# Eighteen weight pieces laid 2,080 bytes apart instead of 2,048

## The chip, the cores and the metric

The kernel runs on one core of one Trainium2 chip. The metric is the device time of that core in microseconds (us), taken as the median of several runs. Data lives in three places: the chip's main memory, the on-chip working memory (128 partitions, each a row of bytes with its own addresses), and the accumulators that TensorE (PE) writes. VectorE (DVE), ScalarE (ACT) and GpSimd (POOL) work beside PE, and SyncE (SP) issues the transfers. PEld in the profile is PE's loading of weights, which goes on beside its matmuls.

## The reference

The program computes an attention with two kinds of masks, and then a feed-forward layer that takes the largest of three products:

```python
scores = scale * np.matmul(q, k.transpose(0, 1, 3, 2))      # q, k, v: 8 x 8 heads x 576 x 64
scores = np.where(masks[None, :, :, :], scores, -1000000000.0)
attn = np.exp(scores - np.max(scores, axis=-1, keepdims=True))
attn = attn / (np.sum(attn, axis=-1, keepdims=True) + 1e-09)
x = np.matmul(attn, v)                                       # turned to 4608 tokens x 512
h = np.maximum(np.maximum(x @ w1, x @ w2), x @ w3)           # 512 -> 768, three times
out = h @ w_out                                              # 768 -> 512
```

Heads 0 to 3 look back over a window of 32 positions, heads 4 to 7 over 32 positions that lie 4 apart. q, k, v and the output are float32; the four weight matrices come as float64, each number in two words of 32 bits.

## The kernel before, in words

**Stages.** The 4,608 tokens are worked through in nine tiles of 512. Attention makes the columns of x for a tile (in "units" of one half sequence and a pair of heads), and the feed-forward layer of the tile follows. A planner with costs and due times writes all instructions in one order ahead of time, so that the attention of the next tile is woven into the matmuls of this one. For the last two tiles no attention is left.

**Two parts for each operand.** To get near to float32 accuracy from a fast matmul, x, the weights and h are each held as a high part and a low remainder, in a float32 form that PE takes at its faster rate (fp32r, shown as f32 in the rows). A product is three products: high x by high weights, low x by high weights, high x by low weights.

**The up product** (function `ffn`, L828) is the largest part. For each tile, each of six blocks f of 128 hidden columns and each of the three weight matrices g, there are 3 terms times 4 chunks c of 128 inputs: 12 matmuls, 1,944 over the kernel. The weights of a chunk (128 columns, 512 bytes in each partition) are loaded as the stationary operand, and 512 tokens of xH or xL (2,048 bytes in each partition) stream past. Every matmul has a weight load of its own, which runs beside the matmul ahead of it.

**The down product** (L883) has 648 matmuls of the same size. There h is the stationary operand, and the weights wdn stream past.

**Where the up weights lie.** Two tiles, wupH and wupL, hold the high and the low parts. Each has 18 pieces, number j = 3f + g, and a piece is 4 chunks of 512 bytes, one behind the other. The pieces are written once: the float64 words of a piece are brought into a staging tile st by a transfer, made into one float32 each on DVE, ACT and POOL, then cast into wupH (ACT, L346, once DVE, L350) and the remainder subtracted into wupL (POOL, L353). The function `weight` does it; `copy` and `tt` are the helpers whose lines the rows show.

**Addresses.** Tiles that stay for the whole kernel are laid out in order of their making, one behind the other in each partition: ident, identb, masks, wupH, wupL, xH, xL, and then all others. In the built program the starts are these (bytes in each partition, and the remainder by 512 in brackets):

| tile | start before | start after |
|---|---|---|
| masks, identb | 1,920 (384) and 1,664 (128) | the same |
| wupH, piece j | 2,944 + 2,048 j (384) | 2,944 + 2,080 j (384 + 32 j) |
| wupL, piece j | 39,808 + 2,048 j (384) | 40,384 + 2,080 j (448 + 32 j) |
| xH, chunk c | 76,672 + 5,120 c (384) | 77,824 + 5,120 c (0) |
| xL, chunk c | 97,152 + 5,120 c (384) | 98,304 + 5,120 c (0) |
| wdn, the first | 153,376 (288) | 154,528 (416) |
| h, the first | 177,952 (288) | 179,104 (416) |

All the wdn tiles have the remainder 288 before, and all the h tiles too. A matmul starts inside x at a multiple of 1,024 bytes from its chunk's start, and inside wdn or h at a multiple of 512.

Of the kernel before, what the change touches and what calls it, by code (L numbers as in the profile page):

```python
# [9 lines left out]
F32R = mybir.dt.float32r  # L10
# [12 lines left out]
NPAIR = H // 2  # L23
NF = DF // 128
BLOCK = 256
RING = 5 * BLOCK
NEG = -8e9
REBIAS = 2.0**-112
TICK = 10.24 / 3
TILES = [2 * BLOCK] * 9  # L30

# [230 lines left out]
def tile_dilated_window_attention__then__maxout_ffn(  # L262
# [18 lines left out]
    const = ctx.enter_context(tc.tile_pool(name="const", bufs=1))  # L281
# [6 lines left out]

    masks = const.tile([128, 4, 128], BF16, name="masks")
    mask = masks[:, 1]  # L290
    wupH = const.tile([128, 3 * NF, 4, 128], F32R, name="wupH")
    wupL = const.tile([128, 3 * NF, 4, 128], F32R, name="wupL")
    xH = const.tile([128, NPAIR, RING], F32R, name="xH")
    xL = const.tile([128, NPAIR, RING], F32R, name="xL")

# [24 lines left out]
    def buf(tag, name, shape=None, dtype=None):  # L320
        if tag in BANKS:
            return Buf(ps, tag, BANKS[tag], [128, 512], F32, name)
        if tag in KEPT:
            return Buf(KEPT[tag], tag, len(KEPT[tag]), None, None, name)
        n, sh, dt = SIZES[tag]
        return Buf(work, tag, n, shape or sh, dtype or dt, name)
# [17 lines left out]
    def copy(eng, dst, src):  # L344
        if eng == "act":
            nc.scalar.copy(dst, src)  # L346
        elif eng == "pool":
            nc.gpsimd.tensor_scalar(dst, src, 1.0, 1.0, ALU.mult, ALU.mult)
        else:
            nc.vector.tensor_copy(dst, src)  # L350
# [5 lines left out]
    def act(n, psum=True):  # L356
        return (0.155 if psum else 0.195) + 0.00084 * n

    def dve(n):
        return 0.15 + 0.00105 * n  # L360

    def dve2(n):
        return 0.15 + 0.00053 * n

    def pool1(n):
        return 0.17 + 0.00093 * n

    def pool(n):
        return 0.08 + 0.00245 * n
# [6 lines left out]
    def weight(j, before):  # L376

        up = j < NWU
        n = 512 if up else 256
        if not up:  # L380
            f, n0 = (j - NWU) // 2, n * ((j - NWU) % 2)
        tag = STAGE[j % len(STAGE) if j < STAGE_H else 0] if up else "o"
        st = buf(tag, f"st{j}", [128, 2 * n], F32)
        res = [] if up else [wdn[f]]

        def part(z):
            if up:
                return (wupL if z else wupH)[:, j].rearrange("p c m -> p (c m)")
            return wdn[f].t[:, z, n0 : n0 + n]

        cb, cp = buf("tmp", f"c{j}"), buf("b", f"cp{j}")

        def high():
            return st.t.rearrange("p (n t) -> p n t", t=2)[:, :, 1]

        def cf():
            return cb.t[:, :n]

        def cw():
            return cb.t.bitcast(U32)[:, :n]  # L400

        def pf():
            return cp.t[:, :n]

        def pw():
            return cp.t.bitcast(U32)[:, :n]

        def rebias(e):  # L410

            if e == "act":
                nc.scalar.mul(pf(), high(), REBIAS)
            else:
                nc.vector.tensor_scalar(pf(), high(), REBIAS, None, ALU.mult)

        def low3(e):

            b = st.t.bitcast(U8).rearrange("p (n t) -> p n t", t=8)[:, :, 3]
            (nc.gpsimd if e == "pool" else nc.vector).tensor_scalar(cw(), b, 1 / 32, -31 / 64, ALU.mult, ALU.add)  # L420

        def joined(_):

            nc.vector.scalar_tensor_tensor(
                pw(), pw(), 3, cw(), op0=ALU.logical_shift_left, op1=ALU.bitwise_or
            )

        def split(e):
            copy(e, part(0), cf())

        def sign(_):
            nc.vector.scalar_tensor_tensor(
                cw(), st.t.bitcast(U32).rearrange("p (n t) -> p n t", t=2)[:, :, 1], 0x80000000, pw(), op0=ALU.bitwise_and, op1=ALU.bitwise_or
            )

        s = plan.add(
            {"sp": 0.5},
            lambda _: nc.sync.dma_start(out=st.t.bitcast(I64), in_=w_up[j] if up else w_dn[j - NWU]),
            bufs=[st],
            nbytes=128 * 8 * n,  # L440
        )
        first = plan.add({"act": act(n, False), "dve": dve(n)}, rebias, [s, before], [st, cp])
        s = plan.add({"pool": pool1(n), "dve": dve(n)}, low3, [s, before], [st, cb])
        s = plan.add({"dve": dve(n)}, joined, [s, first], [cp, cb])
        s = plan.add({"dve": dve(n)}, sign, [s], [st, cp, cb])
        s = plan.add({"act": act(n, False), "dve": dve2(n), "pool": pool1(n)}, split, [s], [cb, *res])
        l = plan.add(
            {"pool": pool(n), "dve": dve(n)},
            lambda e: tt(e, part(1), cf(), part(0).bitcast(F32), ALU.subtract),
            [s],  # L450
            [cb, *res],
        )
        return s, l, first
# [160 lines left out]
    def rounded_of(half, p, dil, pv):  # L614

        r0 = (half * HALF) % RING
        cut = min(HALF, RING - r0)
        parts = [(0, cut, r0)] + ([(cut, HALF, 0)] if cut < HALF else [])
# [184 lines left out]
    def ffn(t0, n, x_of, w_of, prev):  # L803

        r0 = t0 % RING
        turned = r0 + n > RING

        def moving(x, c):

            if turned:  # L810
                return x[:, c].rearrange("p (b k) -> p b k", k=BLOCK)[:, 0 : RING // BLOCK : RING // BLOCK - 1]
            return x[:, c, r0 : r0 + n]

        def sums(bank):
            return bank.t[:, :n].rearrange("p (b k) -> p b k", k=BLOCK) if turned else bank.t[:, :n]

        halves = range(t0 // HALF, -(-(t0 + n) // HALF))
        hs, hsteps = [], []
        for f in range(NF):
            tmp, hb = buf("tmp", f"tmp{t0}_{f}"), buf("h", f"h{t0}_{f}")  # L820
            for g in range(3):
                bank = buf("ffn", f"u{t0}_{f}_{g}")
                terms = ((wupH, 0, 0), (wupH, 0, 1), (wupL, 1, 0))
                for m, (wt, wz, xz) in enumerate(terms):

                    def up(_, m=m, wt=wt, xz=xz, f=f, g=g, bank=bank):
                        for c in range(4):
                            nc.tensor.matmul(  # L828
                                sums(bank),
                                wt[:, 3 * f + g, c, :],  # L830
                                moving(xL if xz else xH, c),
                                start=(m == 0 and c == 0),
                                stop=(m == 2 and c == 3),
                            )

                    prev = plan.add(
                        {"pe": 4 * (n * 0.000425 + 0.01)},
                        up,
                        [
                            prev,  # L840
                            *(x for h in halves for p in range(NPAIR) for x in x_of[h, p][xz]),
                            w_of[3 * f + g][wz],
                        ],
                        [bank],
                    )
                if g == 0:
                    s = plan.add(
                        {"act": act(n), "dve": dve(n)},
                        lambda e, bank=bank, tmp=tmp: copy(e, tmp.t[:, :n], bank.t[:, :n]),
                        [prev],  # L850
                        [bank, tmp],
                    )
                else:
                    s = plan.add(
                        {"dve": dve(n)},
                        lambda e, bank=bank, tmp=tmp: tt(e, tmp.t[:, :n], bank.t[:, :n], tmp.t[:, :n], ALU.max),
                        [prev, s],
                        [bank, tmp],
                    )
            a = plan.add(  # L860
                {"act": act(n, False), "dve": dve2(n), "pool": pool1(n)},
                lambda e, tmp=tmp, hb=hb: copy(e, hb.t[:, 0, :n], tmp.t[:, :n]),
                [s],
                [tmp, hb],
            )
            l = plan.add(
                {"pool": pool(n), "dve": dve(n)},
                lambda e, tmp=tmp, hb=hb: tt(
                    e, hb.t[:, 1, :n], tmp.t[:, :n], hb.t[:, 0, :n].bitcast(F32), ALU.subtract
                ),  # L870
                [a],
                [tmp, hb],
            )
            hs.append(hb)
            hsteps.append((a, l))
        last_up = prev
        for s0 in range(0, n, 128):
            bank, o = buf("ffn", f"d{t0}_{s0}"), buf("o", f"o{t0}_{s0}")
            for f in range(NF):
# [25 lines left out]
                {"sp": 0.5},  # L905
                lambda _, q0=t0 + ((s0 + BLOCK) % n if turned else s0), o=o: nc.sync.dma_start(out=out[q0 : q0 + 128], in_=o.t),
                [s],
# [116 lines left out]
```

## Time and profile before

| | |
|---|---|
| median of three runs | 722.84 us (722.43 to 723.27) |
| the profiled execution | 724.2 us, of which 722.3 us lie between its first and last instruction |
| mean granted clock of PE | 0.990 |
| PE busy, of the span | 99% |
| DVE, ACT, POOL busy | 51%, 41%, 32% |

The busy time of PE alone says little, since matmuls are pipelined and the shown end of each is modelled: a matmul is shown as 389 ns long while the next one starts 227 ns later. The distance between the starts of matmuls is therefore the thing to read, and the chain of waits, which follows the work that ended last back to the start.

### The profile page before, as it was taken

The numbers are of one execution on the slowest core, as the hardware profiler recorded it, in microseconds if no ns is written. First come the engines' busy times: TensorE is split into PE (matmuls) and PEld (weight loads), VectorE is DVE, ScalarE is ACT, GpSimd is POOL, SyncE is SP. The second block draws the span as 40 slices with busy tenths as digits, with TensorE's granted clock in tenths as the row PEclk, the third lists the DMA queues.
The fourth block names the chain that finished last, engine by engine and source line by source line (L and its number), as shares of the span: only waits on it lengthen the run. The fifth ranks groups of instructions, "written<-read, shape, count | busy, mean of one in ns | idle before, by whom it ended". The sixth has DMA issues, their size and how long they took to land.

```text
span 722.3 us, 12780 instructions
## 1 busy us (share of the span) xinstructions
PE 712.2 (99%) x4534; PEld 578.2 (80%) x4539; DVE 371.7 (51%) x1456; ACT 294.5 (41%) x1101; POOL 231.9 (32%) x328
## 2 busy tenths in 40 slices
PE   8899999999999999999999999999999999999997
PEld 4577878888888888888888888888888888888886
DVE  5978966556556554655456555655555511101110
ACT  4866763334444444444434334434343411111111
POOL 3888762233223332322222222332223301200110
PEclk9969999999999999999999999999999999999999
DMA  8991532211222223212321222112220010000001
GB/s 262 344 325 49 185 101 93 75 32 58 89 89 63 59 78 102 63 59 64 103 77 60 63 76 92 49 37 80 87 64 25 15 44 0 1 29 30 1 0 59
DMA packets 31232, 57.45 MB, mean 80 GB/s; under 512 B 3008, under 2 KB 11200, under 8 KB 31168
## 3 DMA queue, kind: packets, MB, share of 16 engines
q1 hardware_dynamic: 31168, 56.64, 24.4%
q8 instruction: 36, 0.59, 0.3%
q14 instruction: 28, 0.23, 0.1%
HBM read 47.19 MB, written 9.44 MB: 78 GB/s over the span
## 4 chain that ended last, share of the span: by engine, by line
PE 95%; POOL 2%; DVE 1%; DMA 1%; issue 0%; SPq 0%; ACT 0%; POOLq 0%; ACTq 0%; DVEq 0%
PE u L828 62%; PE d L883 21%; PE s L670 5%; PE pv L776 4%; PE s L509 1%; DMA st<-in_w_up_dram 1%; POOL W L353 1%; PE pt L590 1%; PE pv L604 1%; PE idle L962 0%; POOL wupL L353 0%; PE s L504 0%; DVE mx L527 0%; DVE sm L544 0%; POOL c L420 0%
## 5 line engine op out<-in xcount | busy, mean ns | idle before, releaser
L353 DVE TENSOR_TENSOR tmp<-u,tmp 128x512 f32<-128x512 f32 x108 | 74.7, 691 | 206.6 <-PE u L828 190.0
L828 PE MATMUL u<-xL,wupH 128*128 128x512 f32 x648 | 176.3, 394 | 0.0
L828 PE MATMUL u<-xH,wupH 128*128 128x512 f32 x648 | 175.4, 393 | 0.0
L828 PE MATMUL u<-xH,wupL 128*128 128x512 f32 x648 | 174.1, 390 | 0.0
L883 PE MATMUL d<-wdn,h 128*128 128x512 f32 x648 | 150.8, 391 | 0.0
L353 POOL TENSOR_TENSOR h<-tmp,h 128x512 fp32r<-128x512 f32 x54 | 69.7, 1290 | 244.6 <-ACT h L346 244.6
L693 ACT ACTIVATE W<-W,mx 96x128 f32<-96x128 f32 (+3 forms) x364 | 134.1, 371 | 27.0 <-DVE mx L702 25.9
L828 PEld LDWEIGHTS u<-xH,wupL 128*128 128x128 f32 x648 | 121.4, 188 | 25.9
L883 PEld LDWEIGHTS d<-wdn,h 128*128 128x128 f32 x648 | 121.1, 188 | 26.3
L828 PEld LDWEIGHTS u<-xH,wupH 128*128 128x128 f32 x648 | 121.4, 189 | 25.8
L828 PEld LDWEIGHTS u<-xL,wupH 128*128 128x128 f32 x648 | 120.9, 189 | 26.4
L764 DVE STREAM_TRANSPOSE PT<-W 32x192 f32<-32x192 f32 (+1 forms) x312 | 124.7, 400 | 32.3 <-POOL W L353 28.1
L346 ACT CAST h<-tmp 128x512 fp32r<-128x512 f32 x54 | 33.4, 619 | 208.9 <-DVE tmp L353 208.8
L353 POOL TENSOR_TENSOR W<-W,sm 96x384 f32<-96x384 f32 (+3 forms) x125 | 99.2, 812 | 45.2 <-DVE sm L743 40.3
L702 DVE CUSTOM_DVE_ANT_0 W<-s,masks 96x128 f32<-96x128 f32 (+3 forms) x364 | 70.1, 257 | 52.6 <-PE s L670 52.6
L693 ACT ACTIVATION_READ_ACCUMULATOR W<-W,mx 72x1 f32 (+1 forms) x364 | 68.6, 189 | 0.0
L738 POOL TENSOR_TENSOR sm<-sm,small_c 96x6 f32<-96x6 f32 (+1 forms) x52 | 10.3, 198 | 166.3 <-ACT W L693 166.1
L346 ACT COPY tmp<-u 128x512 f32<-128x512 f32 x54 | 31.7, 587 | 67.9 <-PE u L828 51.2
L346 ACT COPY o<-d 128x512 f32<-128x512 f32 x36 | 21.1, 587 | 82.3 <-PE d L883 75.3
L670 PE MATMUL s<-k 64*96 64x128 f32 (+3 forms) x728 | 38.7, 254 | 0.0
L670 PEld LDWEIGHTS s<-k 64*72 64x72 f32 (+1 forms) x728 | 33.7, 149 | 2.8 <-ACT tmp L346 0.4
L776 PEld LDWEIGHTS pv<-PT,v 104*64 104x64 f32 (+1 forms) x728 | 27.2, 137 | 9.2 <-issue 8.8
(56 smaller groups left out, 410.9 us busy)
## 6 DMA issues: line engine op xcount, KB each, us to landing
k<-in_qk_d_dram SPq DMA_DIRECT2D x32, 352.0 KB, 3.0
k<-in_qk_p_dram SPq DMA_DIRECT2D x32, 304.0 KB, 3.2
st<-in_w_up_dram SPq DMA_DIRECT2D x18, 512.0 KB, 10.4
out_dram<-o SPq DMA_DIRECT2D x36, 256.0 KB, 2.0
v<-in_v_d_dram SPq DMA_DIRECT2D x32, 208.0 KB
v<-in_v_p_dram SPq DMA_DIRECT2D x32, 192.0 KB, 6.1
st<-in_w_dn_dram SPq DMA_DIRECT2D x12, 256.0 KB, 2.6
```

Source lines behind the costliest of these rows:

```text
L346: nc.scalar.copy(dst, src)
L353: (nc.vector if eng == "dve" else nc.gpsimd).tensor_tensor(dst, a, b, op=op)
L509: nc.tensor.matmul(S3(j)[:nq, i], kb.t[d, nq * i : nq * i + nq], kb.t[d, k0 : k0 + wk], start=False, stop=True, skip_group_check=True,)
L590: nc.tensor.transpose(bank.t[:wk, nq * i : nq * i + nq], W3()[:nq, nb * j + i], ident[:nq, :nq])
L670: nc.tensor.matmul(banks[j].t[:nq, wk * i : wk * i + nk], kb.t[d, q0 : q0 + nq], kb.t[d, k0 : k0 + nk], start=True, stop=True,)
L693: nc.scalar.activation(a, a, AF.Exp, bias=mx.t[:nq, n : n + 1], scale=-1.0, accum_out=sm.t[:nq, n : n + 1])
L702: nc.vector.tensor_tensor_reduce(W3()[:nq, n, mo : mo + nk], banks[j].t[:nq, wk * i : wk * i + nk], mask[:nq, mo : mo + nk], -0.125, 3e38, ...
L738: nc.gpsimd.tensor_tensor(a, a, eps_c[:nq].broadcast_to([nq, 2 * nb]), op=ALU.add)
L764: nc.vector.transpose(PT.t[c : c + 32, : 2 * nb, 32 * i : 32 * i + 32], W3(e)[32 * i : 32 * i + 32, :, c - e : c - e + 32],)
L776: nc.tensor.matmul(pv.t[64 * j : 64 * j + 64, q0 : q0 + nq], v.t[:wk, j, i, :], PT.t[:wk, nb * j + i, :nq], start=True, stop=True,)
L828: nc.tensor.matmul(sums(bank), wt[:, 3 * f + g, c, :], moving(xL if xz else xH, c), start=(m == 0 and c == 0), stop=(m == 2 and c == 3),)
L883: nc.tensor.matmul(bank.t, hs[f].t[:, hz, s0 : s0 + 128], wdn[f].t[:, wz], start=(f == 0 and m == 0), stop=(f == NF - 1 and m == 2),)
```

## The change

The two weight tiles are made flat, with 520 elements (2,080 bytes) for each piece, and are then seen as 18 pieces of which the first 512 elements are used. The 8 elements behind each piece are never written nor read. Each tile grows by 18 x 32 = 576 bytes, so wupL starts 576 bytes later and all tiles behind it 1,152 bytes later; the table above has the starts. The slices at the two places of use name the same elements in other words. The 7,025 instructions stay the same, in number, in kind, in their order on every engine and in what each waits for; only the addresses in them differ. The accumulators' addresses do not change.

```diff
+PIECE = 520
...
-    wupH = const.tile([128, 3 * NF, 4, 128], F32R, name="wupH")
-    wupL = const.tile([128, 3 * NF, 4, 128], F32R, name="wupL")
+    wupH = const.tile([128, 3 * NF * PIECE], F32R, name="wupH").rearrange("p (j x) -> p j x", x=PIECE)[:, :, :512]
+    wupL = const.tile([128, 3 * NF * PIECE], F32R, name="wupL").rearrange("p (j x) -> p j x", x=PIECE)[:, :, :512]
...
         def part(z):
             if up:
-                return (wupL if z else wupH)[:, j].rearrange("p c m -> p (c m)")
+                return (wupL if z else wupH)[:, j]
...
                             nc.tensor.matmul(
                                 sums(bank),
-                                wt[:, 3 * f + g, c, :],
+                                wt[:, 3 * f + g, 128 * c : 128 * c + 128],
                                 moving(xL if xz else xH, c),
```

## The prediction

> **What bounds the kernel now.** I read the chain of waits first, then the distance between matmuls. On the page, the busy times and the chain:
>
> ```profile
> span 722.3 us, 12780 instructions
> PE 712.2 (99%) x4534; PEld 578.2 (80%) x4539; DVE 371.7 (51%) x1456; ACT 294.5 (41%) x1101; POOL 231.9 (32%) x328
> PE 95%; POOL 2%; DVE 1%; DMA 1%; issue 0%; SPq 0%; ACT 0%; POOLq 0%; ACTq 0%; DVEq 0%
> PE u L828 62%; PE d L883 21%; PE s L670 5%; PE pv L776 4%; PE s L509 1%; DMA st<-in_w_up_dram 1%; POOL W L353 1%; PE pt L590 1%; PE pv L604 1%; PE idle L962 0%; POOL wupL L353 0%; PE s L504 0%; DVE mx L527 0%; DVE sm L544 0%; POOL c L420 0%
> ```
>
> The reader is to see that 95% of the chain is PE, and that the up product, whose weights the change moves, is 62% of it. So whatever a single up matmul gains or loses is gained or lost 1,944 times on the path that sets the end. The question is thus one number: the distance between two up matmuls, and whether the addresses set it.
>
> The timeline of PE in the last tile, where no attention is woven in, gives this number. One row is four matmuls (start in us, us, then what it is):
>
> ```profile
> 655.85 1.07 PE L828 MATMUL u<-xH,wupH 128*128 128x512 f32 x4
> 656.76 1.07 PE L828 MATMUL u<-xL,wupH 128*128 128x512 f32 x4
> 657.66 1.07 PE L828 MATMUL u<-xH,wupL 128*128 128x512 f32 x4
> ...
> 699.37 1.07 PE L828 MATMUL u<-xH,wupH 128*128 128x512 f32 x4
> 700.28 1.07 PE L828 MATMUL u<-xL,wupH 128*128 128x512 f32 x4
> ```
>
> From 655.85 to 700.28 there are 49 such groups, 196 matmuls, one every 44.43 / 196 = 226.7 ns. These are the pieces j = 1 to 17, high and low parts, both x tiles. The three rows of piece 1 start 0.91 and 0.90 us apart, those of piece 17 0.91.
>
> The chain gives the down product beside it, in the same tile:
>
> ```profile
> 653.25 49.02 PE u L828 x216
> 702.26 16.38 PE d L883 x72
> ```
>
> 49.02 / 216 = 226.9 ns for up, 16.38 / 72 = 227.5 ns for down, a start-up included in each. So two products whose operands lie in quite different tiles keep the same distance.
>
> What this distance has over the bare stream shows in the idle matmuls at the start, which are bf16 and have 512 columns and a weight load each too. The timeline there, and the next matmul behind them:
>
> ```profile
> 10.94 1.03 PE L962 MATMUL idle<-masks,identb 128*128 128x512 bf16 x4 [0.16 <-issue]
> 11.80 0.34 PE L504 MATMUL s<-masks,identb 96*96 96x416 bf16 x1
> ```
>
> (11.80 - 10.94) / 4 = 215 ns, or 216 within the rounding of the two starts. The fp32r matmul thus takes 226.7 - 216 = 10.7 ns more, and this excess is what an address could at best take away.
>
> **The change part by part.** Nothing is added, removed or reordered, so each part is a duration that could differ by its address.
>
> *The up matmuls, 1,944 of them.* What changes is how the weight chunk lies to the x that streams at the same time. Before, both starts leave the remainder 384 by 512, so their distance is a multiple of 512: by 2,048 it takes each of 0, 512, 1,024 and 1,536, since the chunk c steps by 512 in the weights and by 5,120 in x. The four matmuls of one row above are four such distances in a row, and 49 rows keep the same pace to 0.01 us. At steps of 512 bytes the distance therefore costs nothing. Finer than 512, before shows no fp32r matmul at all, since wdn and h share their remainder too. After, the distance takes every multiple of 32; it stays a multiple of 512 only for piece 4 of wupH (72 matmuls over nine tiles: 8 in each) and piece 2 of wupL (36), so 1,944 - 108 = 1,836 matmuls change. The bounds are: gain 1,836 x 10.7 ns = 19.6 us, if all of the excess is a collision that the spreading ends; loss the same size, if the excess were doubled instead. I take 0, since nothing in the rows moves with the address, neither between the four chunks nor between pieces nor between up and down.
>
> *The weight loads.* A chunk of an odd piece will start 32 bytes past a multiple of 64; before, all up weights start on one (384 = 6 x 64). The rows of the two tiles:
>
> ```profile
> L828 PEld LDWEIGHTS u<-xH,wupH x648: 186/188/338, 45.2 to 699.8; 128*128 128x128 f32 x162
> L883 PEld LDWEIGHTS d<-wdn,h x648: 186/188/189, 110.6 to 718.0; 128*128 128x128 f32 x162
> ```
>
> (The three figures are least, median and largest, in ns.) The loads from h already start 32 past a multiple of 64 (288 = 4 x 64 + 32) and take the same 188 ns. So the term is 0, and beneath it lies a cover: the load runs beside the matmul ahead of it, 226.7 - 188 = 38.7 ns shorter. Should the cover go, each ns beyond it costs 972 ns for the half of the matmuls that have odd pieces.
>
> *Writing the pieces.* 18 casts and 18 subtractions write to the new addresses, once. From the views of the four tiles:
>
> ```profile
> L353 POOL TENSOR_TENSOR wupL<-c,wupH x18: 1263/1287/1603, 21.9 to 67.4; 128x512 fp32r<-128x512 f32 x18
> L353 POOL TENSOR_TENSOR h<-tmp,h x54: 1264/1288/1602, 58.1 to 703.8; 128x512 fp32r<-128x512 f32 x54
> L346 ACT CAST wupH<-c x17: 603/622/666, 20.0 to 65.7; 128x512 fp32r<-128x512 f32 x17
> L346 ACT CAST h<-tmp x54: 607/620/621, 56.1 to 703.0; 128x512 fp32r<-128x512 f32 x54
> ```
>
> The same operations with h, 32 bytes past a multiple of 64, differ by +1 and -2 ns in the median. 18 x 1 ns less 18 x 2 ns is -0.02 us, and of these writes only those on the chain count (0% for POOL wupL). I take 0, between -0.1 and +0.1 us.
>
> *The shift of all other tiles by 1,152 bytes.* 1,152 is 18 x 64, so what starts on or off a multiple of 64 stays so. k, v, W, PT, h, wdn and st move together and keep their distances to each other; to x too they shift by nothing, since x moves by the same 1,152. What changes is their distance to ident, masks and the up weights. The transfers into st are the only ones on the chain, with 1% of it, about 7 us, and they run beside matmuls at 95% of the DMA engines' time:
>
> ```profile
> 0.00:45.00 45.00, 38.70 (x352) 25.03 (x357) 33.72 (x84) 30.58 (x104) 30.11 (x48) 0.89 0.95 319
> ```
>
> (window, length; busy us of PE, PEld, DVE, ACT and POOL; then PE's granted clock, the DMA share and GB/s.) If a row of bytes at another start cost 2% more, that would be 0.14 us. I take 0, between -0.15 and +0.15 us.
>
> *The sum.* 0 + 0 + 0 + 0. A profiled execution of the changed kernel should again show a span near 722.3 us and a time near 724.2. That one run lies 1.4 us (0.2%) above the median of the others, so the forecast stands on the median: 722.84 us, rounded to 722.8.
>
> **The rivals.**
>
> *B, faster: the excess is a collision of PE's two reads.* For it speaks that the fp32r stream reads twice the bytes of a bf16 one, that the excess is there in fp32r alone, and that before every fp32r matmul without exception has its two operands at a distance of a multiple of 512, so a collision at equal places would strike all alike and show exactly this even pace. Also x will start on a multiple of 512 for the first time. Against it: two streams that advance at different rates (128 columns in 188 ns, 512 in 227) pass through all distances within a single matmul, so that the start should matter little, and the distances 0 to 1,536 are equal. If it holds, the gain is up to 19.6 us on PE's chain, 722.8 - 19.6 = 703.2 us; the down product keeps its 227 ns. The Trainium skill's "TensorE: Matmul & The Clock Gate", section "Back-to-back issue gap", gives N / 2.4 + 2.5 ns between warm matmuls, an estimate of 215.8 ns for 512 columns. The idle matmuls agree with it at 216 ns, the fp32r ones do not at 226.7 ns, and by the formula 10.9 ns in each would be avoidable. The skill's "SBUF — State Buffer", section "Door 1: The DMA port swizzle", has the engines' banks made of groups of four partitions, by which no spacing along a partition could bring a collision; no run here shows the banks.
>
> *C, slower: the weight load at a start off 64 outgrows its cover.* The place is the load of the odd pieces, half of the up matmuls. It decides from 188 + 38.7 = 226.7 ns on. One more line of 64 bytes to read beside eight would make it 188 x 9 / 8 = 211.5 ns, still hidden, and the time stays. If each line were read twice, 376 ns, 149 ns would be laid bare 972 times, 145 us, and the time would be 868 us. The loads from h speak against both. What they do not show is such a start in the weights under a stream that begins on a multiple of 512, as x now does; a collision that this brings, of the size of the excess, gives 722.8 + 19.6 = 742.4 us.
>
> *D, the change moves only the start.* Before 45 us PE waits for the weights and its clock is still rising (0.89 in the row above), so a few ns in a transfer can place the rise differently. The two bounds above, 0.25 us together, are the price: 722.6 to 723.1 us, which a measurement cannot tell from the forecast.
>
> **How the numbers follow.** A 0.81 and D 0.04 (722.8), B 0.10 (703.2, in part something between), C 0.05 (742.4). About 0.2%, 1.4 us, is what a measurement of this kernel can tell from no change; the three runs before spread over 0.84 us. So faster by more has 0.10, within it 0.85, slower by more 0.05. The range follows from A and D alone, as B and C together are less than 2 in 10: the bounds of the small terms (0.25 us) and the spread of the runs around their median (0.4 us) are widened to the 0.2% for another chip or hour, 721.4 to 724.2 us.
>
> **What would show it.** In the profile of the changed kernel, the rows of the last tile should again start 0.91 us apart, for even and odd pieces alike, weight loads should have a median of 188 ns, and the chain should give the last 216 up matmuls 49.0 us. If instead the up groups start 0.86 us apart (4 x 216 ns) while the 72 down matmuls keep 16.4 us, B is right. If LDWEIGHTS of wupH shows a median over 200 ns, or a largest value above 227 ns past the first 50 us, C's place is seen. If pieces differ from each other, with piece 4 of wupH at another pace than its neighbours, addresses do count at a grain finer than 512, and the step that failed is my zero for the up matmuls.

## The result, and the profile after

The changed kernel takes 732.69 us (median; 732.22 to 733.49), the kernel before 723.06 us in the runs beside it. The ratio is 1.0134, with a 95% interval of 1.0117 to 1.0152: **slower by 9.6 us**. The forecast was no change, 721.4 to 724.2 us, and the measured time lies outside this range.

The page of the changed kernel, its busy times and its chain:

```profile
span 730.3 us, 12780 instructions
PE 716.5 (98%) x4534; PEld 573.6 (79%) x4539; DVE 374.6 (51%) x1456; ACT 294.9 (40%) x1101; POOL 231.9 (32%) x328
PE 91%; POOL 3%; DVE 2%; DMA 2%; issue 1%; ACT 0%; SPq 0%; POOLq 0%; DVEq 0%; ACTq 0%
```

PE still carries the chain. Its last part, which in the kernel before read 49.02 us for the 216 up matmuls and 16.38 us for the 72 down matmuls:

```profile
660.13 50.22 PE u L829 x216
710.35 16.35 PE d L884 x72
```

The up product of this tile is 1.20 us longer, 232.5 ns for each matmul in place of 226.9. The down product differs by 0.03 us. By the starts of the single matmuls in the two traces, each of the last two tiles loses 1.2 us, and each of the six ahead of them, into which attention is woven, 1.07 to 1.09 us; these eight together lose 8.9 us. The first tile starts at different times in the two executions and can't be compared in this way.

The timeline of PE in the same tile (start, length, what) shows where:

```profile
668.30 1.10 PE L829 MATMUL u<-xH,wupH 128*128 128x512 f32 x4
669.24 1.10 PE L829 MATMUL u<-xL,wupH 128*128 128x512 f32 x4
670.18 1.09 PE L829 MATMUL u<-xH,wupL 128*128 128x512 f32 x4
671.11 1.07 PE L829 MATMUL u<-xH,wupH 128*128 128x512 f32 x4
672.02 1.07 PE L829 MATMUL u<-xL,wupH 128*128 128x512 f32 x4
672.92 1.10 PE L829 MATMUL u<-xH,wupL 128*128 128x512 f32 x4
673.86 1.09 PE L829 MATMUL u<-xH,wupH 128*128 128x512 f32 x4
```

Groups of four now start 0.93 or 0.94 us apart in these rows, where in the kernel before they were 0.907 us apart (44.43 / 49). Two groups keep the old pace: those from 671.11 and 672.02. They are piece 4 of wupH, the one piece of wupH that still lies a multiple of 512 bytes from x. The weight loads themselves and the writes of the pieces are as before:

```profile
L829 PEld LDWEIGHTS u<-xH,wupH x648: 186/188/192, 42.2 to 707.9; 128*128 128x128 f32 x162
L354 POOL TENSOR_TENSOR wupL<-c,wupH x18: 1260/1294/1613, 21.5 to 66.1; 128x512 fp32r<-128x512 f32 x18
L347 ACT CAST wupH<-c x17: 606/622/663, 19.2 to 64.3; 128x512 fp32r<-128x512 f32 x17
```

One thing must be taken out before the spans are compared. They differ by 8.0 us, not 9.6, because the profiled execution of the kernel before lost time at its start. The first 45 us of the kernel changed, in the columns used before:

```profile
0.00:45.00 45.00, 36.35 (x359) 22.64 (x364) 35.98 (x85) 31.45 (x107) 30.27 (x48) 1.00 0.97 331
```

PE's granted clock is 1.00 here and was 0.89 there; the first up matmul starts at 42.2 us here and at 45.2 us there. The lower clock is not a property of that kernel: 37 further executions of it, run beside the experiments below, have mean granted clocks of 0.998 to 1.000, where the profiled one has 0.990.

### The profile page after: what moved, and what is told of

Read it like the earlier page. It is cut to its first block, busy times and chain, and to the rows that moved or that the text cites. A ratio compares the mean times of both kernels' runs of the same rounds, so it can differ in the third digit from the quotient of the medians.

```text
span 730.3 us, 12780 instructions
## 1 busy us (share of the span) xinstructions
PE 716.5 (98%) x4534; PEld 573.6 (79%) x4539; DVE 374.6 (51%) x1456; ACT 294.9 (40%) x1101; POOL 231.9 (32%) x328
## 4 chain that ended last, share of the span: by engine, by line
PE 91%; POOL 3%; DVE 2%; DMA 2%; issue 1%; ACT 0%; SPq 0%; POOLq 0%; DVEq 0%; ACTq 0%
PE u L829 60%; PE d L884 20%; PE s L671 5%; PE pv L777 4%; DMA st<-in_w_up_dram 2%; POOL wupL L354 2%; POOL c L421 1%; PE s L510 0%; DVE mx L528 0%; PE idle L963 0%; DVE W L354 0%; PE pv L605 0%; DVE c L433 0%; POOL W L354 0%; PE pt L591 0%
## 5 line engine op out<-in xcount | busy, mean ns | idle before, releaser
L829 PE MATMUL u<-xL,wupH 128*128 128x512 f32 x648 | 178.6, 397 | 0.9 <-DVE xL L354 0.9
L829 PE MATMUL u<-xH,wupH 128*128 128x512 f32 x648 | 178.0, 396 | 0.0
L829 PE MATMUL u<-xH,wupL 128*128 128x512 f32 x648 | 177.5, 396 | 0.0
```

Of the source, the lines that this page charges most:

```text
L829: nc.tensor.matmul(sums(bank), wt[:, 3 * f + g, 128 * c : 128 * c + 128], moving(xL if xz else xH, c), start=(m == 0 and c == 0), stop=(m ...
```

## The experiments

All distances below are those of a weight chunk to the x that streams past, in bytes, weights minus x (for the down product h minus wdn, since h is the operand that is loaded there). Three theories stood against each other. OWN: a matmul pays for the distance that it has. CHANGE: it pays when the distance differs from that of the matmul ahead of it. START: it is x at a multiple of 512 that costs.

### One distance for 36 matmuls in a row

```diff
+OFF = [0, 0, 0, 32, 32, 32, 64, 64, 64, 96, 96, 96, 128, 128, 128, 160, 160, 160]
-    wupH = const.tile([128, 3 * NF, 4, 128], F32R, name="wupH")
-    wupL = const.tile([128, 3 * NF, 4, 128], F32R, name="wupL")
+    wup = [const.tile([128, 9344], F32R, name=f"wup{z}") for z in "HL"]
+    wupH, wupL = ([t[:, 512 * j + OFF[j] // 4 :][:, :512] for j in range(3 * NF)] for t in wup)
```

The tiles have 512 bytes of room, so that wupL and x keep their remainder of 384. The other two of this kind have other offsets.

> Pieces 2,048 bytes apart within a block f, x where it was by 512; the weights of block f lie 0, 32, 64, 96, 128, 160 bytes past x by 512, high and low parts alike, so that 36 matmuls in a row keep one distance. Theory OWN (each matmul pays for the distance between its weights and the stream): block 0 keeps 226.7 ns, the blocks at 32, 96 and 160 stay near 233 ns for all 36, those at 64 and 128 near 229 to 232; time near 731.5 us. Theory CHANGE (a matmul pays only when the distance changes from the one ahead of it): every block falls back to 226.7 ns within some nine matmuls, as after a break in the kernel before (587.70 to 589.56 us, 46 ns in all); time 724 to 726 us. Theory START (it is x beginning on a multiple of 512, not the weights): all blocks 226.7 ns, time 722.8 us.

> As d_low with distances 192, 224, 256, 288, 320, 352. OWN: 224, 288 and 352 near 233 ns, 192 and 320 near 231, 256 near 227 to 229, time near 731 us. CHANGE: all back to 226.7 ns, 724 to 726 us. START: 226.7 ns and 722.8 us.

> As d_low with distances 16, 384, 416, 448, 480, 512. OWN: 512 is 226.7 ns if the pattern repeats by 512, 416 and 480 near 233, 384 and 448 near 231, 16 unknown (226.7 if lines of 32 bytes or more decide, else slower); time near 731 us. CHANGE: all back to 226.7 ns, 724 to 726 us. START: 226.7 ns and 722.8 us.

Measured: 732.24, 732.11 and 731.28 us, one run each, beside 723.4 us for the kernel before. The timeline of PE in the run with distances 0 to 160 (one row at the start of each block, and two inside the block at distance 0):

```profile
595.11 1.07 PE L829 MATMUL u<-xH,wupL 128*128 128x512 f32 x4
...
600.55 1.08 PE L829 MATMUL u<-xH,wupL 128*128 128x512 f32 x4
601.46 1.09 PE L829 MATMUL u<-xH,wupH 128*128 128x512 f32 x4
...
609.86 1.10 PE L829 MATMUL u<-xH,wupH 128*128 128x512 f32 x4
...
618.26 1.09 PE L829 MATMUL u<-xH,wupH 128*128 128x512 f32 x4
...
626.68 1.09 PE L829 MATMUL u<-xH,wupH 128*128 128x512 f32 x4
...
635.05 1.09 PE L829 MATMUL u<-xH,wupH 128*128 128x512 f32 x4
...
643.45 9.72 PE L884 MATMUL d<-wdn,h 128*128 128x512 f32 x42
```

At distance 0, 24 matmuls take 600.55 - 595.11 = 5.44 us, 226.7 ns each. The blocks behind it have 36 each: 32 takes 8.40 us (233.3 ns), 64 takes 8.40, 96 takes 8.42 (233.9), 128 takes 8.37 (232.5), 160 takes 8.40. Nothing falls back to 226.7 ns within the block, so CHANGE falls, and x keeps its remainder of 384 by 512, so START falls.

The run with 192 to 352 shows the repeat. Timeline of PE around its block at 256:

```profile
601.84 1.09 PE L829 MATMUL u<-xH,wupH 128*128 128x512 f32 x4
...
609.30 1.09 PE L829 MATMUL u<-xH,wupL 128*128 128x512 f32 x4
610.23 1.07 PE L829 MATMUL u<-xH,wupH 128*128 128x512 f32 x4
611.14 1.07 PE L829 MATMUL u<-xL,wupH 128*128 128x512 f32 x4
...
617.48 1.08 PE L829 MATMUL u<-xH,wupL 128*128 128x512 f32 x4
618.40 1.09 PE L829 MATMUL u<-xH,wupH 128*128 128x512 f32 x4
619.32 1.10 PE L829 MATMUL u<-xL,wupH 128*128 128x512 f32 x4
...
626.79 1.09 PE L829 MATMUL u<-xH,wupH 128*128 128x512 f32 x4
```

The block at 224 (from 601.84) takes 8.39 us, that at 256 (from 610.23) 8.17 us, 226.9 ns each, that at 288 (from 618.40) 8.39 us. So 256 is as good as 0, from its first group on. On the way out, the last group still at 256 already takes 0.92 us: by the single starts in the trace its last matmul is 235 ns long, where the ones ahead are 226 or 227. On the way in it is the other way round: the last matmul at 224 is already 226 ns long, where those ahead of it in its block are 230 to 235. The matmul that changes first is thus the one beside which the first weight load of the next block runs, which points to the load that runs beside a stream, and not to the weights in use.

The paces of all scans, from the starts of the blocks in the second tile from the end (36 matmuls each; distance by 256; the figure at 0 is from the block at 512, since that at 0 contains the tile's start-up; the one at 192 contains it too, and the block at 448, which does not, has 228.9):

| distance | 0 | 32 | 64 | 96 | 128 | 160 | 192 | 224 |
|---|---|---|---|---|---|---|---|---|
| ns | 226.9 | 233.1 | 233.4 | 234.0 | 232.5 | 233.2 | 229.1 | 233.1 |

Distances 288, 320 and 352 gave 233.1, 233.3 and 233.9 ns, and 384, 416, 448, 480 and 512 gave 232.4, 233.1, 228.9, 233.2 and 226.9 ns. That is the row of 32 to 224 and 0 again to 0.2 ns, so the pattern repeats by 256. In the changed kernel piece j lies 128 + 32 j (wupH, two thirds of the matmuls) and 192 + 32 j (wupL) from x by 256. The mean of the table over these is 232.0 ns, and (232.0 - 226.9) x 1,944 = 9.9 us, beside the measured loss of 9.6 us. The match is partly luck: the table's paces come from 36 matmuls at one distance, while the changed kernel changes its distance every 4 or 8 matmuls, and its last tile has 232.5 ns; 0.5 ns for each matmul are 1.0 us over the kernel.

### Which part of the change does it

x alone was moved by 128 bytes, with the weights 2,048 bytes apart:

```diff
+    const.tile([128, 32], F32, name="xpad")
     xH = const.tile([128, NPAIR, RING], F32R, name="xH")
```

> Pieces 2,048 bytes apart as before, x alone 128 bytes further, to a multiple of 512; one distance (384) for all 1,944 up matmuls. OWN: all near 231.5 ns, (231.5 - 227.4) x 1,944 = 8 us, time 731 us. CHANGE: 226.7 ns, time 722.8 us, no change. START: as the change itself, 732.7 us.

Measured: 734.61 us beside 723.4, ratio 1.0155 (1.0135 to 1.0174). The last tile's chain reads

```profile
662.07 50.40 PE u L830 x216
```

or 233.3 ns for all. A single wrong distance in the whole kernel costs more than the spread of the change.

The scans had 232.5 ns at 128 and 232.4 at 384, which is the distance here, so the distance alone does not fix the pace. By the single starts, this run alternates between 229 and 237 or 238 ns, while the two scans run through a longer cycle from 228 to 241 ns. Both cycles occur in one execution at the same addresses: in the run with distances 0 to 160, the block at 128 alternates between 229 and 238 ns in the third tile, which has attention woven into it, and runs through the long cycle in the tile before last. What went ahead thus also counts, here for 0.9 ns in each matmul.

The pitch of 2,080 bytes alone, with x at its old remainder:

```diff
+OFF = [32 * j for j in range(18)]
+    wup = [const.tile([128, 9472], F32R, name=f"wup{z}") for z in "HL"]
```

> The pitch of the change alone: pieces 2,080 bytes apart, but wupL and x kept at the remainder 384 by room behind the weights, so that piece j of both tiles lies 32 j past x. DISTANCE with a repeat of 256, from the paces of the scans (0: 226.9, 32: 233.1, 64: 233.4, 96: 233.9, 128: 232.5, 160: 233.2, 192: 229.1, 224: 233.1 ns), weighted by how many of the 18 pieces have each: 231.7 ns, (231.7 - 226.9) x 1,944 = 9.3 us over 723.3, time 732.6 us. If the change's loss came from x moving to a multiple of 512: 723.3 us.

Measured: 731.68 us beside 723.0, ratio 1.0118 (1.0102 to 1.0135). That is 8.7 us where the scans foresaw 9.3. Each half of the change spoils the distance on its own; they do not add, since it is the resulting distance that counts.

### Distance, not address and not pitch

128 bytes ahead of the weights move the weights and x together to a multiple of 512:

```diff
+    const.tile([128, 32], F32, name="front")
     wupH = ...
```

> 128 empty bytes ahead of the weights: weights and x all start on a multiple of 512, and their distance is 0 by 512 for all pieces, as before. Theory DISTANCE (only how weights and stream lie to each other counts): 226.7 ns, 722.8 us, no change. Theory ABSOLUTE (it is where x or the weights start): near 232 ns, as in x_shift, 732 us or more.

Measured: 723.03 us beside 723.33, ratio 0.9997 (0.9988 to 1.0007). The last 216 up matmuls take

```profile
651.37 49.02 PE u L830 x216
```

as before. The address alone does nothing.

Pieces as unevenly spread as in the change, but by multiples of 256:

```diff
+OFF = [0, 0, 0, 256, 256, 256, 512, 512, 512, 768, 768, 768, 768, 768, 768, 1024, 1024, 1024]
+    wup = [const.tile([128, 9472], F32R, name=f"wup{z}") for z in "HL"]
```

> x as before; the six blocks of pieces lie 0, 256, 512, 768, 768 and 1,024 bytes past it by 2,048, so pieces are as unevenly spread as in the change, but every distance is a multiple of 256. DISTANCE with a repeat of 256: 226.7 ns everywhere, 722.8 us, no change. If the spreading of the pieces itself costs (CHANGE of distance, or any pitch other than 2,048): blocks that follow a step run slower, 724 to 732 us.

Measured: 723.48 us beside 723.33, ratio 1.0002 (0.9992 to 1.0012), and again 49.02 us for the last 216:

```profile
652.33 49.02 PE u L829 x216
```

A pitch other than 2,048 costs nothing as long as it leaves the distance a multiple of 256.

### Not of the up product alone

```diff
-        "wd": (NF, [128, 2, DM], F32R),
+        "wd": (NF, [128, 2 * DM + 8], F32R),
...
-            return wdn[f].t[:, z, n0 : n0 + n]
+            return wdn[f].t[:, DM * z + n0 : DM * z + n0 + n]
```

(and the other uses of these tiles cut to their first elements in the same way)

> Up weights and x as before. The wdn tiles are 4,128 bytes apart, so the six blocks of the down product have h at 192, 32, 96, 64, 128 and 160 past wdn by 512. DISTANCE (any fp32r matmul pays): the down product goes from 227.2 to about 232.5 ns, 648 x 5.3 = 3.4 us, time 726.3 us; up stays at 226.7 ns. If it were something of the up tiles alone: 722.8 us.

Measured: 725.86 us beside 723.33, ratio 1.0036 (1.0023 to 1.0048). The chain of its last tile:

```profile
655.12 48.96 PE u L828 x216
704.08 16.74 PE d L883 x72
```

The down product of this tile is 0.36 us longer than before, 232.5 ns for each matmul. The up product, whose addresses are as before, is 0.06 us shorter: behind the down product its first nine matmuls take 224 to 236 ns in the kernel before, and 226 or 227 ns here. Nine tiles at 0.36 - 0.06 = 0.30 us are 2.7 us; 2.5 us arrive in the median. So the down product pays as well, with other tiles and with h as the loaded operand.

### Finer distances

> The blocks lie 4, 8, 12, 248, 252 and 260 bytes past x by 512. If the collision is between whole lines of 16 bytes or more, 4, 8, 12 and 260 still run at 226.7 ns or between, 248 and 252 slower; if the single word decides, all are near 233 ns, time near 732 us. A distance that gives 216 ns, as bf16 has, would be a way to beat both kernels; no theory foresees one.

> A search for a distance that beats 226.7 ns: the blocks lie 60, 124, 188, 220, 236 and 244 bytes past x by 256. If the pattern is that of the multiples of 32 with 4 bytes of play, as 252 runs like 0, then 60 is like 64 (233.4), 124 like 128 (232.5), 188 like 192 (229.1), 220 like 224 (233.1), and 236 and 244 near 233; time near 731 us. A pace under 226.7 ns in any block would make a kernel that beats both; no theory foresees it.

The edit is another OFF. Measured: 728.47 us (4, 8, 12, 248, 252, 260) and 731.59 us (60 to 244), one run each. The paces from the block starts are 232.2 ns at 4, 230.7 at 8, 233.2 at 12, 233.1 at 248, 226.9 at 252 and 232.2 at 260; then 230.6 at 60, 233.3 at 124, 233.3 at 188, 233.4 at 220, 231.5 at 236 and 233.2 at 244; the scan above had 233.3 at 16. So a single word of 4 bytes decides, against the idea of lines, and 260 equals 4, which is the repeat by 256 again. Only 0 and 252 keep 226.7 ns. The guess that 4 bytes less make no difference holds for 252 and, to 0.3 ns, for 220; 60 is 2.8 ns from 64, 124 is 0.8 ns from 128, and 188 is 4.2 ns from 192. Of the 20 distances by 256 that the five scans tried, none is under 226.7 ns, so none of them makes a kernel faster than the one before.

### What the load's size does

In the first of these two, the third term alone used 64 of its 128 weight columns; in the second, all matmuls but the first of each sum, as shown here. Both leave out a part of the product.

```diff
+                            cols = 64 if m or c else 128
                             nc.tensor.matmul(
-                                sums(bank),
-                                wt[3 * f + g][:, 128 * c : 128 * c + 128],
+                                sums(bank)[:cols],
+                                wt[3 * f + g][:, 128 * c : 128 * c + cols],
```

> Distances 0, 32, 64, 128, 192, 256 by block; the third term (wupL) loads and uses only 64 of its 128 weight columns, so half of that part of the product is left out. Theory READS (the weight load's reads hold up the stream's): the four matmuls of the third term have about half of the excess over 216 ns, 221 ns at distances 0 and 256 and 224 ns at the others, the first two terms as in the scans. Theory HANDOVER (a fixed cost for each change of weights, whatever its size): the third term is as slow as the others, 226.7 and 229 to 233 ns.

> Eleven of the twelve matmuls of each sum load and use 64 of 128 weight columns (the other half of that part of the product is left out); distances 0, 32, 64, 128, 192, 256 by block. Theory READS (the stream is held up for as long as the load beside it reads): settled pace about 221 ns at 0 and 256 and 224 ns elsewhere, time near 717 us. Theory FIXED (a collision holds the stream up by an amount that the load's size does not set): 226.7 ns at 0 and 256, 229 to 234 elsewhere, 730 us. Beside it identb lies 32 bytes further from masks by 256: if bf16 matmuls pay for the distance too, the idle matmuls before 14 us are over 216 ns apart, else 216 ns.

Measured: 729.93 us and 727.36 us, one run each. In the first, the third term of the last tile takes 230.0, 230.8, 232.5, 231.2, 228.4 and 230.6 ns for each matmul in the six blocks, by the single starts: nowhere the 221 or 224 ns of READS, and at 0 and 256 not the 226.7 ns of HANDOVER either. From the second, the view of the tile u and the timeline of PE (the rows at the start of the blocks at 0, 32, 64, 128, 192 and 256):

```profile
L832 PEld LDWEIGHTS u<-xL,wupH x648: 132/134/138, 42.6 to 703.9; 128*64 128x64 f32 x162
```

```profile
655.52 1.09 PE L832 MATMUL u<-xH,wupH 128*128 128x512 f32 x4
...
663.80 1.09 PE L832 MATMUL u<-xH,wupH 128*128 128x512 f32 x4
...
672.14 1.09 PE L832 MATMUL u<-xH,wupH 128*128 128x512 f32 x4
...
680.50 1.09 PE L832 MATMUL u<-xH,wupH 128*128 128x512 f32 x4
...
688.83 1.08 PE L832 MATMUL u<-xH,wupH 128*128 128x512 f32 x4
...
697.05 1.07 PE L832 MATMUL u<-xH,wupH 128*128 128x512 f32 x4
...
705.32 0.86 PE L888 MATMUL d<-wdn,h 128*128 128x512 f32 x3
```

The loads are shorter, 134 ns for 188, and yet the blocks take 8.28, 8.34, 8.36, 8.33, 8.22 and 8.27 us, 230.0, 231.7, 232.2, 231.4, 228.3 and 229.7 ns for each matmul. READS, in the simple form that the excess is in proportion to what the load reads, falls: nowhere is 221 ns. At 32 to 192 the pace is 0.8 to 1.4 ns better than in the scans. FIXED does not fit either at 0 and 256, where the pace got worse, 230 ns for 226.7. In the single starts at distance 0 by 256 the matmuls run through 224, 227, 234, 230, 236 and 229 ns and do not settle. One reading is that 226.7 ns is a rhythm that a load and a stream fall into only when all loads are alike and the distance is a multiple of 256; these two runs, in which full loads are mixed in, do not prove it. What a load and a stream contend for stays open.

The same run had identb 32 bytes further from masks by 256. Its 14 idle bf16 matmuls in a row read

```profile
12.24 3.20 PE L967 MATMUL idle<-masks,identb 128*128 128x512 bf16 x14
```

and 14 take 3.20 us in the kernel before too (its row at 13.12 us). The bf16 matmul does not pay for this distance, one distance tried.

## Why the prediction was wrong

**Right:** that PE's chain makes whatever a single up matmul gains or loses into the result; the distance between matmuls as the number to read; the count of 1,836 matmuls that change their distance (108 fewer lose, 1,728, since piece 12 of wupH and piece 10 of wupL lie at 256, which is as good as 512); the weight loads at 188 ns wherever they start; the writes of the pieces (622 and 1,294 ns after, 622 and 1,287 before); nothing from the shift of the other tiles, as far as it was tried: with the up distances kept at multiples of 256, a shift by 128 bytes gave a ratio of 0.9988 to 1.0007 (weights and x moved together) and one by 2,048 bytes 0.9992 to 1.0012 (the spread by 256). The shift by 1,152 bytes was not run alone.

**Wrong:** one step, "I take 0" for the up matmuls. The working had seen that no fp32r matmul of the kernel before lies at a distance finer than 512, wrote that such distances were not shown, and then took the even pace at 0, 512, 1,024 and 1,536 as a sign that the address does not matter. It was a sign of nothing: all four are the same place by 256. The second argument, that two streams at different rates pass through all distances anyway and the start should matter little, was an argument without a row, and the scans refute it: 4 bytes make 226.9 into 232.2 ns. The last of the signs that the prediction had named is the one that came: piece 4 of wupH keeps another pace than its neighbours.

**The sign.** The even pace made me look for the collision in the kernel before (rival B, 0.10), with the spreading as its cure. It was the other way round: 0 by 256 is, with 252, the best of the 20 distances tried, and the kernel before had it everywhere, for up and down alike, because the starts of its two operands lie multiples of 512 bytes apart in both. Whether it was chosen or fell out so is not in the profile; the forecast should have asked what an edit does to a place where everything is aligned. Rival C had the right side and, in its last sentence, nearly the right mechanism (a collision that the new distances bring, on top of the excess) at 0.05 and 742.4 us. Its size was taken as the whole excess, 10.7 ns; measured are 5.1 ns in the mean of the scans, hence half of the 19.6 us. Its first mechanism, a longer weight load, did not happen.

**An inference from a page.** "SBUF — State Buffer" of the Trainium skill, section "Door 1: The DMA port swizzle", describes the engines' banks as groups of four partitions. That no spacing along a partition could bring a collision was my own conclusion from it, which the section does not draw. The runs with x moved by 128 bytes (1.0155) and with both moved (0.9997) show that the spacing of the two operands along the partition does count; the measurement decides. The formula in "TensorE: Matmul & The Clock Gate" of the Trainium skill, section "Back-to-back issue gap", which stands there for a single warm matmul, gives an estimate of 215.8 ns for 512 columns. The bf16 matmuls of this case agree with it at 216 ns; the fp32r matmul is above it at every distance tried, by 10.9 ns at best.

**The clock before 45 us.** Rival D read the 0.89 of the kernel before as a clock that is still rising. Read in smaller windows, the same profile has 1.00 in the first 27 us, 0.50 from 36 to 45 us and 1.00 from 54 us on: a dip in that execution. The forecast did not hang on it.

**The range.** It was drawn from the small terms and the spread of runs, though the bounds of the one term that carried the question, +19.6 and -19.6 us, stood in the text and had been excluded by argument, not by a row at a finer distance than 512.

## What to carry to other kernels

A pace that is the same for all addresses a kernel uses says nothing about the addresses it does not use: before costing a layout edit at nothing, work out by which power of two all present distances agree. For fp32r matmuls of this size (128 weight columns, 512 stream columns) with a weight load each, keep the start of the weights a multiple of 256 bytes from the start of the stream beside them in the partition; padding that broke this cost 1 to 3% of each matmul at every distance tried but 252. A new pitch or a moved tile cost nothing here as long as it kept that distance.

## What the hardware showed that was not expected

- The pace of fp32r matmuls with 128 weight columns and 512 stream columns depends on the distance of their two operands by 256 bytes: 226.9 ns at 0, 229 to 234 ns at the other multiples of 32.
- It depends on single words: 232.2 ns at 4 bytes, 226.9 ns at 252.
- Distances apart from 0 and 252 do not settle on one number but mostly run through short cycles. In the single starts of the trace, 231 and 235 ns alternate at 32, 236 and 231 at 64, and 226, 229 and 232 follow each other at 192. At 128 two cycles occur at the same addresses, one of 233.3 ns in the mean and one of 232.4.
- Halving the weight columns shortens the load from 188 to 134 ns and brings no block near 221 ns: the pace goes from 226.7 to 230 ns at 0, and from 233.4 to 232.2 ns at 64.
